# Single-token attention mixed with an MLP: one row of wo moves from SP's queue to GpSimd's, and the GpSimd transfers become eleven

## The chip, the core and the metric

The kernel runs on one core of a Trainium2 chip. The core has a matrix engine (PE, with a separate loader of weights, PEld), a vector engine (DVE), a scalar engine (ACT), a general engine (POOL, or GpSimd) and SP, which only issues transfers. Sixteen DMA engines move data between the chip's memory and the core's SBUF of 128 partitions. The metric is the device time of one execution in microseconds, the median of several.

## The reference: what is computed

One token `x` of 512 values goes through two branches, and a gate mixes them.

```python
g = sigmoid((x * gate_w).sum(-1))
# branch a: 32 heads of 128, a cache of 4096 keys and values for each head
q = (x @ wq).reshape(1, 1, 32, 128)
p = softmax(q . k_cache * 128 ** -0.5)
a = (p . v_cache).reshape(1, 1, 4096) @ wo
# branch b
b = relu(x @ w1 + b1) ** 2 @ w2 + b2
out = g * a + (1 - g) * b
```

All inputs are bf16. The caches of keys and values have 32 MB each, `wq` and `wo` 4 MB each, `w1` and `w2` 1.4 MB each. Every byte is read once and used for one token, and the profile counts 78.35 MB read.

## The kernel before

**Tiles and stages.** The heads are taken in `NT` = 8 groups of four. A group's keys or values are one tile of 128 partitions by 16384 elements (4 MB), one of five slots of `ring`. Each partition holds 32 KB of one head. For a group, DVE multiplies one part of the key blocks with the query and sums (`ttr`, L711), and PE transposes the other part (L509), which ACT copies (L415) and PE multiplies with the query (L522). Then come the maximum, the exponentials on ACT (L434) and the products with V on PE (`pv`, L553).

**The order of the loads.** SP's queue first brings `wq` into `W` (L294). Then it goes through `LOADS`: K0, K1, K2, V0, then K3, V1 and so on. Ahead of each load `free` waits until the slot's former tile has been used. Ahead of the fifth entry, K3, SP waits in `started` until the queries are done, since then `W`, which held `wq`, is free for `wo`. The values of the last three groups come in parts (`PARTS`, L331), with a semaphore each. `w1` and `w2` (L336, L337) come before the last values. The last things on SP's queue are the wo rows of the last four heads (`wob`, L339), the last 128 rows of `w2` (L341) and, at the end, the store of the output (L343).

**Where wo lies.** The first 28 heads' part of `wo` is 3584 rows of 512. It is held as 112 rows of 16384 elements, 32 KB each, on 112 of the 128 partitions of `W`; which row lies on which partition is free, because a matrix of ones and zeros, `selA`, spreads the heads' outputs to match. GpSimd builds `selA` with one `affine_select` for each strip of rows.

A strip is a transfer of `k` rows to `k` partitions at a step. The code counts the sixteen DMA engines as `e` = 0 to 15. Its function `place` turns a kind, an engine, a number of engines, an offset `r` and a multiple `m` into the first partition, the step and the number of rows: `INNER` is 32 + 4e + r, `OUTER` is 4e + r for e below 8 and 64 + 4e + r from 8 on. So the code counts eight partitions as an engine's own: four `INNER` and four `OUTER`. `SEAM` joins partition 28 + r with 96 + r (engines 7 and 8), and `WRAP` joins r with 124 + r (engines 0 and 15).

There are two lists. `FIRST` is issued by SP, ahead of K3, on the semaphore `s_wr` (L327): seven strips of three rows, on engines 0 to 2, and one strip of a single row, `(OUTER, 4, 1, 3, 1)`, which is partition 19. `RUNS` is issued by GpSimd (L378): fourteen strips, each with a semaphore of its own from `s_wp`. A GpSimd transfer of `k` rows takes the next `k` engines from a cursor. To bring the cursor to `e`, `turns` counts how far it has to move, and GpSimd issues a small transfer into `dm` of as many rows (L375); seven of them are issued. A row in a GpSimd strip goes as two pieces of 16 KB (`max_dma_last_dim=16384`).

By these lists, rows for each engine before: engines 0, 1 and 2 have eight each on their own partitions (seven from `FIRST`, one from `RUNS`), engine 3 has none, 4 to 6 and 9 to 14 have seven, and 7, 8 and 15 have eight. The single row of partition 19 is counted for none of these; partition 19 is one of those that the code counts as engine 4's.

**Who waits for wo.** After its last issue GpSimd waits for all `dm` and `wo` transfers and then writes `tick` (L386). PE (`spread_a`) and DVE (`rows_v`) wait for that. PE multiplies 22 of the 32 row columns of `W` (L580) and DVE takes the other ten (L773, L777). PE adds DVE's sum (L586), the last group's `pv` follows, then `norm` (L741), the last four heads' wo (`out_b`, L614) and the last part of w2 (`mlp_out`, L605). DVE adds the bias (L814), PE turns the result (L667), DVE copies it (L816) and SP stores it.

Of the kernel before, what the change touches and what calls it, by code (L numbers as in the profile page):

```python
# [5 lines left out]
def bass_gated_mix__gqa_block_cached__dense_activation_squared_relu__decode_kernel(  # L6
# [50 lines left out]
    for i in (28, 29, 30):  # L57
# [19 lines left out]
    TV = 10  # L77
    TP = 32 - TV
    TM = 6
    INNER, OUTER, SEAM, WRAP = range(4)  # L80
    RUNS = [(INNER, 4, 12, 0, 2), (INNER, 4, 12, 1, 2),
            (OUTER, 4, 3, 0, 1), (SEAM, 7, 2, 0, 1), (OUTER, 9, 7, 0, 1), (OUTER, 4, 3, 1, 1),
            (SEAM, 7, 2, 1, 1), (OUTER, 9, 7, 1, 1), (OUTER, 4, 3, 2, 1),
            (SEAM, 7, 2, 2, 1), (OUTER, 9, 7, 2, 1),
            (SEAM, 7, 2, 3, 1), (WRAP, 15, 2, 3, 1), (OUTER, 1, 2, 3, 1)]
    FIRST = [(INNER, 0, 3, 0, 1), (INNER, 0, 3, 1, 1), (INNER, 0, 3, 2, 1), (INNER, 0, 3, 3, 1),
             (OUTER, 0, 3, 0, 1), (OUTER, 0, 3, 1, 1), (OUTER, 0, 3, 2, 1),
             (OUTER, 4, 1, 3, 1)]

    def place(kind, e, k, r, m):  # L90
        if kind == INNER:
            return 32 + 4 * e + r, 4 // m, k * m
        if kind == OUTER:
            return (4 * e if e < 8 else 64 + 4 * e) + r, 4, k
        if kind == SEAM:
            return 28 + r, 68, k
        return r, 124, k

    def turns():
        at, out = 0, []  # L100
        for _, e, k, _, _ in RUNS:
            d = (e - at) % 16
            out.append((False, d) if d != 1 else (True, e))
            at = (e + k) % 16
        return out

    def strips():
        q = 0
        for run in RUNS + FIRST:
            yield (*place(*run), q)  # L110
            q += place(*run)[2]
        assert q == 4 * NA

    STRIPS = list(strips())
# [4 lines left out]
    woa_v = A_wo.rearrange("(p t) n -> p (t n)", t=32)  # L119
# [15 lines left out]
    with ctx:  # L135
        def sb(name, shape, dt):
            return ctx.enter_context(nc.sbuf_tensor(name, shape, dt))
# [4 lines left out]
        def sem(name):  # L142
            return ctx.enter_context(nc.semaphore(name))
# [3 lines left out]
        def held(kind, j=0):  # L147
            return ring[:, AT[kind, j] % SLOTS, :]

        W = sb("W", [128, 32 * DM], bf16)  # L150
# [90 lines left out]
        s_wp = [sem(f"s_wp{n}") for n in range(len(RUNS))]  # L241
        s_dm = [sem(f"s_dm{n}") for n in range(len(RUNS))]
        s_wr = sem("s_wr")
# [56 lines left out]
        def free(eng, n):  # L300
            if n < SLOTS:
                return
            kind, j = LOADS[n - SLOTS]
            if kind == "k":
                eng.wait_ge(s_sd, U * (j + 1))
                eng.wait_ge(s_t, 2 * U * (j + 1))
            elif kind == "v":
                eng.wait_ge(s_pv, U * (j + 1))

        def started(eng):
            eng.wait_ge(s_qps, NT)
            eng.wait_ge(s_g, 4)
            eng.wait_ge(s_b1c, 1)

        @block.sync
        def _(eng):
            for n, (kind, j) in enumerate(LOADS):
                free(eng, n)  # L320
                if n == SLOTS - 1:
                    started(eng)
                    for p, st, k, q in STRIPS[len(RUNS):]:
                        a, b = W[p:p + st * (k - 1) + 1:st, :], woa_v[q:q + k, :]
                        if k == 1:
                            a, b = [v.rearrange("p (a n) -> p a n", a=2) for v in (a, b)]
                        eng.dma_start(a, b).then_inc(s_wr, 16)  # L327
                if kind == "v" and j in PARTS:
                    for w in range(len(PARTS[j]) - 1):
                        part = slice(PARTS[j][w] * 128, PARTS[j][w + 1] * 128)  # L330
                        eng.dma_start(held("v", j)[:, part], v_v[j][:, part]).then_inc(s_vl[j, w], 16)  # L331
                elif kind in "kv":
                    eng.dma_start(held(kind, j), (k_v if kind == "k" else v_v)[j])\
                       .then_inc(s_l[n % SLOTS], 16)
                elif kind == "m":
                    eng.dma_start(held("m")[:, 0:W2], w1_v).then_inc(s_w[0], 16)  # L336
                    eng.dma_start(held("m")[:, W2:W3], w2_v).then_inc(s_w[1], 16)  # L337
            for c in range(len(TS) - 1):
                eng.dma_start(wob_sb[:, TS[c]:TS[c + 1], :], wob_v[:, TS[c]:TS[c + 1], :])\  # L339
                   .then_inc(s_wo[c], 16)  # L340
            eng.dma_start(w2b, B_w2[F - 128:F, :]).then_inc(s_w[2], 16)  # L341
            eng.wait_ge(s_f4, 1)
            eng.dma_start(out[0, 0, :].rearrange("(j p) -> j p", p=128), fin4).then_inc(s_out, 16)  # L343

        @block.gpsimd
        def _(eng):
            eng.memset(ident[:, :], 0.0).then_inc(s_id, 1)
            eng.memset(identf[:, :], 0.0).then_inc(s_id, 1)
            eng.memset(onesf[:, :], 1.0).then_inc(s_cst, 1)  # L350
            eng.wait_ge(s_id, 2)
            for m in (ident, identf):
                eng.affine_select(out=m[:, :], in_=m[:, :], compare_op=ALU.not_equal, fill=1.0,
                                  base=0, pattern=[[-1, 128]], channel_multiplier=1)\
                   .then_inc(s_id, 1)
            eng.memset(RS[:, :], 0.0).then_inc(s_cst, 1)
            eng.memset(E[:, :, :, :], 0.0).then_inc(s_cst, 1)
            eng.memset(selA[:, :, :], 0.0).then_inc(s_sel, 1)
            eng.wait_ge(s_sel, 1)
            for n, (p, st, k, q) in enumerate(STRIPS):  # L360
                eng.wait_ge(s_sel, n + 1)
                part = selA[:, :, p:p + st * (k - 1) + 1]
                eng.affine_select(out=part, in_=part, compare_op=ALU.not_equal, fill=1.0, base=-st * q,
                                  pattern=[[st, 4], [-1, st * (k - 1) + 1]], channel_multiplier=4 * st)\
                   .then_inc(s_sel, 1)

            started(eng)
            sent = 0
            for n, ((back, d), run) in enumerate(zip(turns(), RUNS)):  # L370
                if back:
                    eng.inc_swdge_sem([], [], mode="reset_dge_cursor")
                if d:
                    src = B_w1[0:d, 0:32].rearrange("p (a c) -> p a c", a=2)
                    eng.dma_start(dm[0:d, sent, :, 0:4], src[:, :, 0:4]).then_inc(s_dm[sent], 16)  # L375
                    sent += 1
                p, st, k, q = STRIPS[n]
                eng.dma_start(W[p:p + st * (k - 1) + 1:st, :], woa_v[q:q + k, :],  # L378
                              max_dma_last_dim=16384).then_inc(s_wp[n], 16)
            for n in range(sent):  # L380
                eng.wait_ge(s_dm[n], 16)
            eng.wait_ge(s_wr, 16 * len(FIRST))
            for q in s_wp[:-1]:
                eng.wait_ge(q, 16)
            eng.wait_ge(s_wp[-1], 16)
            eng.memset(tick[:, :], 0.0).then_inc(s_wk, 1)  # L386
# [461 lines left out]
```

## Time and profile before

| | |
|---|---|
| runs | 193.02, 193.01, 193.13 us; median 193.02 |
| profiled execution | 192.9 us, of it a span of 191.5 us from the first to the last instruction |
| busy, share of the span | DVE 83%, PE 58%, PEld 51%, ACT 43%, POOL 12% |
| DMA | 78.74 MB in 5488 packets, mean 411 GB/s |
| granted PE clock | 0.581 in the mean |
| SP's wo transfers (L327) | 8, issued from 33.5 us on, 411 to 806 ns each |
| GpSimd's wo transfers (L378) | 14, issued from 34.5 to 45.5 us, 556 to 615 ns each |

The page gives busy times of the engines, then the span in 40 slices with one digit each (9 is 90% or more busy), then the DMA queues: q1 has what SP issues, q0 what GpSimd issues, q10 what ACT issues, and q8 and q14 fetch instructions. The chain of waits follows the work that ended last back in time. A row of the timeline has its start, its length, engine, line, operation, tiles, shapes, and in brackets how long the engine was idle before it and what ended that.

### The profile page before, as it was taken

The page shows a single profiled execution, that of the slowest core. Times are in us where ns is not written, and L with a number is a line of the kernel's source. Part 1 is how long each engine was busy: PE and PEld are TensorE (multiplying, and loading weights), DVE is VectorE, ACT ScalarE, POOL GpSimd, SP SyncE. Part 2 cuts the span into 40 slices and gives each one's busy share as a digit, 9 for nine tenths or more (in the row PEclk, how much of TensorE's full clock was granted, in tenths as well). Part 3 has the DMA queues.
Part 4 walks back from the last instruction along what each step waited for, and adds up shares of the span by engine and source line. Part 5 has one row for each costly group of instructions (what it writes and reads, how often), then busy time and mean ns, then how long its engine had stood idle before and what let it go on. Part 6 is the DMA issues. An engine that isn't in the chain of part 4 may idle for free.

```text
span 191.5 us, 6005 instructions
## 1 busy us (share of the span) xinstructions
PE 111.0 (58%) x2058; PEld 97.6 (51%) x2058; DVE 159.0 (83%) x1387; ACT 82.7 (43%) x204; POOL 22.7 (12%) x56
## 2 busy tenths in 40 slices
PE   0129667545614653397569145933887478648975
PEld 0123335535503542297459145933877268537964
DVE  0320399999999999899999998998999799998821
ACT  2105765843833663087349222941663393000400
POOL 7760000996000000000000000000000000000000
PEclk9999985855555555555555555555555555555555
DMA  6999999999999999999999999999999999999992
GB/s 226 432 438 438 438 440 428 438 411 450 411 443 411 421 412 421 438 429 431 414 447 421 428 426 428 431 417 424 428 419 424 411 428 409 421 415 428 417 382 70
DMA packets 5488, 78.74 MB, mean 411 GB/s; under 512 B 1285, under 2 KB 1927, under 8 KB 2056
## 3 DMA queue, kind: packets, MB, share of 16 engines
q1 hardware_dynamic: 4484, 75.40, 92.9%
q0 software_dynamic: 960, 2.95, 3.9%
q8 instruction: 16, 0.26, 0.6%
q14 instruction: 14, 0.11, 0.1%
q10 hardware_dynamic: 14, 0.01, 0.0%
HBM read 78.35 MB, written 0.00 MB: 409 GB/s over the span
## 4 chain that ended last, share of the span: by engine, by line
DVE 48%; DMA 40%; SPq 7%; PE 3%; issue 1%; DVEq 0%
DVE ring L711 45%; DMA ring<-in_A_k_cache_dram 26%; DMA ring<-in_A_wo_dram 14%; SPq L331 6%; DVE S L711 2%; PE pO L553 1%; PE KP L509 1%; DVE gm L725 1%; DVE gx L728 0%; PE pM L562 0%; PE pM L534 0%; PE pQ L614 0%; SPq L337 0%; SPq L294 0%; DVE mp L718 0%
## 5 line engine op out<-in xcount | busy, mean ns | idle before, releaser
L711 DVE CUSTOM_DVE_ANT_0 ring<-ring,qb 128x128 bf16<-128x128 bf16 x656 | 140.6, 280 | 2.9 <-DMA ring<-in_A_k_cache_dram 2.9
L415 ACT ACTIVATE kT<-KP 128x768 bf16<-128x768 bf16 (+1 forms) x64 | 46.4, 783 | 48.1 <-PE KP L509 47.8
L509 PE MATMUL KP<-ident,ring 128*128 128x128 bf16 x368 | 43.4, 302 | 23.2 <-DMA ring<-in_A_k_cache_dram 19.9
L711 DVE DVE_READ_ACCUMULATOR2_ANT S<- 128x1 f32 x656 | 49.7, 76 | 0.1
L509 PEld LDWEIGHTS KP<-ident,ring 128*128 128x128 bf16 x368 | 36.0, 140 | 25.9 <-DMA ring<-in_A_k_cache_dram 20.4
L553 PE MATMUL pO<-E,ring 128*128 128x4 bf16 x640 | 19.5, 167 | 2.9 <-DMA ring<-in_A_v_cache_dram 1.9
L553 PEld LDWEIGHTS pO<-E,ring 128*128 128x128 bf16 x640 | 18.7, 105 | 3.4 <-DMA ring<-in_A_v_cache_dram 2.1
L434 ACT ACTIVATE E<-S,nM 32x128 bf16<-32x128 f32 x32 | 18.5, 580 | 0.9
L553 PE MATMUL pX<-E,ring 128*128 128x4 bf16 x384 | 12.0, 167 | 4.6 <-DMA ring<-in_A_v_cache_dram 4.6
L553 PEld LDWEIGHTS pX<-E,ring 128*128 128x128 bf16 x384 | 11.4, 105 | 5.1 <-DMA ring<-in_A_v_cache_dram 4.9
L426 ACT ACTIVATE nM<-pM 128x1 f32<-128x1 f32 x8 | 1.4, 172 | 23.0 <-PE pM L534 23.0
L529 PE MATMUL pM<-identf,mp 128*1 128x128 f32 x8 | 3.1, 384 | 13.0 <-DVE mp L718 13.0
L534 PE MATMUL pM<-onesf,gx 1*128 1x1 f32 x16 | 4.6, 357 | 8.9 <-DVE gx L728 8.9
L534 PEld LDWEIGHTS pM<-onesf,gx 1*128 1x128 f32 x16 | 4.0, 306 | 9.6 <-DVE gx L728 9.6
L522 PE MATMUL pQ<-qcol,kT 128*128 128x4 bf16 x176 | 7.8, 170 | 1.0 <-ACT kT L415 0.9
L522 PEld LDWEIGHTS pQ<-qcol,kT 128*128 128x128 bf16 x176 | 7.6, 111 | 1.4 <-ACT kT L415 1.4
L434 ACT ACTIVATION_READ_ACCUMULATOR E<-S,nM 32x1 f32 x32 | 8.1, 253 | 0.0
L522 PE MATMUL pS<-qcol,kT 128*128 128x4 bf16 x192 | 8.1, 169 | 0.0
L386 POOL MEMSET tick<- 1x1 f32 x1 | 0.1, 88 | 66.8 <-DMA W<-in_A_wo_dram 66.8
L378 POOL DMA_DIRECT2D W<-in_A_wo_dram x14 | 8.0, 572 | 0.0
L529 PEld LDWEIGHTS pM<-identf,mp 128*1 128x1 f32 x8 | 0.7, 92 | 14.2 <-DVE mp L718 14.0
L522 PEld LDWEIGHTS pS<-qcol,kT 128*128 128x128 bf16 x192 | 7.8, 108 | 0.2
(83 smaller groups left out, 97.3 us busy)
## 6 DMA issues: line engine op xcount, KB each, us to landing
ring<-in_A_k_cache_dram SPq DMA_DIRECT2D x8, 4096.0 KB, 30.4
ring<-in_A_v_cache_dram SPq DMA_DIRECT2D x5, 4096.0 KB, 29.7
W<-in_A_wq_dram SPq DMA_DIRECT2D x1, 4096.0 KB, 12.4
ring<-in_A_v_cache_dram SPq DMA_DIRECT2D x2, 2048.0 KB, 27.7
ring<-in_A_v_cache_dram SPq DMA_DIRECT2D x4, 1024.0 KB, 27.5
ring<-in_A_v_cache_dram SPq DMA_DIRECT2D x2, 1280.0 KB, 31.4
W<-in_A_wo_dram POOLq DMA_DIRECT2D x2, 768.0 KB, 17.8
ring<-in_B_w_dram SPq DMA_DIRECT2D x1, 1376.0 KB, 24.8
```

The costliest lines, as they stand in the source:

```text
L331: eng.dma_start(held("v", j)[:, part], v_v[j][:, part]).then_inc(s_vl[j, w], 16)
L378: eng.dma_start(W[p:p + st * (k - 1) + 1:st, :], woa_v[q:q + k, :], max_dma_last_dim=16384).then_inc(s_wp[n], 16)
L415: eng.activation(kT[:, n % NC, 0:HB[u // U] * 128], KP[n % 3][:, 0:HB[u // U] * 128], ACT.Copy).then_inc(s_ev, 1)
L426: eng.activation(nM[:, j:j + 1], MB[:, j:j + 1], ACT.Copy).then_inc(s_nm, 1)
L434: eng.activation(E[rows, j % NE, :, r], S[rows, j % NS, :], ACT.Exp, bias=nM[rows, j:j + 1], scale=SCALE, accum_out=RS[rows, R * j + r:R * ...
L509: mm = eng.transpose(KP[n % 3][:, y * 128:(y + 1) * 128], held("k", j)[:, b * 128:(b + 1) * 128], ident[:, :])
L522: mm = eng.matmul(S2[j % 2][:, c:c + R], kT[:, n % NC, y * 128:(y + 1) * 128], qcol[:, R * j:R * j + R], start=True, stop=True)
L529: eng.transpose(MT[0:1, :], mp[:, j:j + 1], identf[:, :]).then_inc(s_mt, 1)
L534: eng.matmul(MB[:, j:j + 1], gx[0:1, j % 2, :], onesf[0:1, 0:1], start=True, stop=True).then_inc(s_mb, 1)
L553: mm = eng.matmul(O(R * j, R * j + R), held("v", j)[:, b * 128:(b + 1) * 128], E[:, j % NE, b, :], start=(b == 0), stop=(b == B - 1), skip ...
L711: ins = eng.tensor_tensor_reduce(kb, kb, qb[:, j, :], 1.0, 0.0, ALU.mult, ALU.add, S[:, j % NS, b:b + 1])
L725: eng.tensor_reduce(g, MT[0:1, :].rearrange("a (r p) -> a r p", r=R), AX.X, ALU.max)\
```

## The change

Row strips change place between the lists, and the single rows change their form.

- `FIRST` gets `(OUTER, 0, 3, 3, 1)`, partitions 3, 7 and 11, in place of the single row of partition 19. SP issues eight strips of three rows.
- `RUNS` has eleven strips for fourteen. Offsets 0 to 2 have two `OUTER` strips each, of four and eight rows, for three strips before. Offset 3 has a single row on engine 4 (partition 19), the `SEAM` of 7 and 8, and a single row on engine 15 (partition 127). `WRAP` is gone.
- A single row in `RUNS` goes from GpSimd as one piece of `SOLO` = 16381 elements (a prime number). Its last three elements go from SP, on `s_wr`, so two more transfers of six bytes are issued after the eight strips, and GpSimd waits for `s_wr` to reach 16 x 10.
- There are eight cursor moves through `dm` for seven: six of four rows, one of two, one of six.
- The same 112 partitions are filled, with their rows of wo in another order, and `selA` follows. Rows for each engine on its own partitions after: 0, 1, 2, 4, 7, 8 and 15 have eight, 3 has none, the others seven. The instructions of PE, DVE and ACT are the same, in the same order.

```diff
--- before.py
+++ after.py
@@ -77,24 +77,22 @@
     TV = 10
     TP = 32 - TV
     TM = 6
-    INNER, OUTER, SEAM, WRAP = range(4)
+
+    SOLO = 16381
+    INNER, OUTER, SEAM = range(3)
     RUNS = [(INNER, 4, 12, 0, 2), (INNER, 4, 12, 1, 2),
-            (OUTER, 4, 3, 0, 1), (SEAM, 7, 2, 0, 1), (OUTER, 9, 7, 0, 1), (OUTER, 4, 3, 1, 1),
-            (SEAM, 7, 2, 1, 1), (OUTER, 9, 7, 1, 1), (OUTER, 4, 3, 2, 1),
-            (SEAM, 7, 2, 2, 1), (OUTER, 9, 7, 2, 1),
-            (SEAM, 7, 2, 3, 1), (WRAP, 15, 2, 3, 1), (OUTER, 1, 2, 3, 1)]
+            (OUTER, 4, 4, 0, 1), (OUTER, 8, 8, 0, 1), (OUTER, 4, 4, 1, 1), (OUTER, 8, 8, 1, 1),
+            (OUTER, 4, 4, 2, 1), (OUTER, 8, 8, 2, 1),
+            (OUTER, 4, 1, 3, 1), (SEAM, 7, 2, 3, 1), (OUTER, 15, 1, 3, 1)]
     FIRST = [(INNER, 0, 3, 0, 1), (INNER, 0, 3, 1, 1), (INNER, 0, 3, 2, 1), (INNER, 0, 3, 3, 1),
-             (OUTER, 0, 3, 0, 1), (OUTER, 0, 3, 1, 1), (OUTER, 0, 3, 2, 1),
-             (OUTER, 4, 1, 3, 1)]
+             (OUTER, 0, 3, 0, 1), (OUTER, 0, 3, 1, 1), (OUTER, 0, 3, 2, 1), (OUTER, 0, 3, 3, 1)]
 
     def place(kind, e, k, r, m):
         if kind == INNER:
             return 32 + 4 * e + r, 4 // m, k * m
         if kind == OUTER:
             return (4 * e if e < 8 else 64 + 4 * e) + r, 4, k
-        if kind == SEAM:
-            return 28 + r, 68, k
-        return r, 124, k
+        return 28 + r, 68, k
 
     def turns():
         at, out = 0, []
@@ -321,10 +319,10 @@
                 if n == SLOTS - 1:
                     started(eng)
                     for p, st, k, q in STRIPS[len(RUNS):]:
-                        a, b = W[p:p + st * (k - 1) + 1:st, :], woa_v[q:q + k, :]
+                        eng.dma_start(W[p:p + st * (k - 1) + 1:st, :], woa_v[q:q + k, :]).then_inc(s_wr, 16)
+                    for p, st, k, q in STRIPS[:len(RUNS)]:
                         if k == 1:
-                            a, b = [v.rearrange("p (a n) -> p a n", a=2) for v in (a, b)]
-                        eng.dma_start(a, b).then_inc(s_wr, 16)
+                            eng.dma_start(W[p:p + 1, SOLO:], woa_v[q:q + 1, SOLO:]).then_inc(s_wr, 16)
                 if kind == "v" and j in PARTS:
                     for w in range(len(PARTS[j]) - 1):
                         part = slice(PARTS[j][w] * 128, PARTS[j][w + 1] * 128)
@@ -375,11 +373,13 @@
                     eng.dma_start(dm[0:d, sent, :, 0:4], src[:, :, 0:4]).then_inc(s_dm[sent], 16)
                     sent += 1
                 p, st, k, q = STRIPS[n]
-                eng.dma_start(W[p:p + st * (k - 1) + 1:st, :], woa_v[q:q + k, :],
-                              max_dma_last_dim=16384).then_inc(s_wp[n], 16)
+                a, b = W[p:p + st * (k - 1) + 1:st, :], woa_v[q:q + k, :]
+                if k == 1:
+                    a, b = a[:, 0:SOLO], b[:, 0:SOLO]
+                eng.dma_start(a, b, max_dma_last_dim=16384 * (1 + (k == 1))).then_inc(s_wp[n], 16)
             for n in range(sent):
                 eng.wait_ge(s_dm[n], 16)
-            eng.wait_ge(s_wr, 16 * len(FIRST))
+            eng.wait_ge(s_wr, 16 * (len(FIRST) + sum(run[2] == 1 for run in RUNS)))
             for q in s_wp[:-1]:
                 eng.wait_ge(q, 16)
             eng.wait_ge(s_wp[-1], 16)
```

## The prediction

> **What bounds the kernel now.** I read first the slices of the page, then its queues, then the chain of waits, then the timeline of the end, and last the single transfers.
>
> ```profile
> span 191.5 us, 6005 instructions
> DVE  0320399999999999899999998998999799998821
> DMA  6999999999999999999999999999999999999992
> q1 hardware_dynamic: 4484, 75.40, 92.9%
> q0 software_dynamic: 960, 2.95, 3.9%
> q8 instruction: 16, 0.26, 0.6%
> q14 instruction: 14, 0.11, 0.1%
> ```
>
> The DMA row stands at 9 from the second slice to the last but one: the sixteen engines that move data never rest, while DVE, the busiest compute engine, falls to 2 and 1 at the end. q1 is what SP issues, q0 what GpSimd issues, q8 and q14 fetch instructions.
>
> The end of the chain of waits (window from 185 us), the waits of the last PE groups, and the timeline rows of those groups:
>
> ```profile
> 162.59 25.97 DMA ring<-in_A_wo_dram
> 188.56 0.14 issue
> 188.70 0.57 PE pQ L614 x16
> 189.26 0.28 PE pQ L605 x4
> ...
> 186.71 1.44 PE L553 MATMUL pO<-E,ring 128*128 128x4 bf16 x48 [0.66 <-DMA ring<-in_A_v_cache_dram]
> 188.26 0.22 DVE L741 SCALAR_TENSOR_TENSOR onorm<-pO,gcol,rden 128x4 bf16<-128x4 f32 x1 [5.10 <-PE pO L553]
> 188.67 0.51 PEld L614 LDWEIGHTS pQ<-onorm,ring 128*128 128x128 bf16 x16 [0.60 <-DVE onorm L741]
> ```
>
> Every late step waits for data: the last values of V before 186.71, then wo for the last heads, then the last rows of w2. These three come down one queue in this order. So the question is which DMA engine is last, and why.
>
> The views name no engine, but the trace keeps the sixteen arrivals of each completion semaphore, and each packet with start, length, size and queue. The w2 rows' semaphore arrives at 189.22 from the last engine, 188.79, 188.77, 188.75, 188.70, 188.54, 188.45 and 188.38 from the next seven, 188.0 and earlier from eight. Packets can be strung into sixteen engines, since one starts 3 to 4 ns before the former's end, and since the order of sizes on each engine follows from the code (the counts agree: 960 on q0). Strung so, no engine is idle between 2 us and its own last packet. What an engine carries is its finish. Last packets end:
> - engine 0: 188.80. It carries nine rows of wo (32 KB each), eight on its own partitions and the lone row of partition 19.
> - engines 5, 6 and 9 to 14: seven rows each and the fetches of q8, two each before their data end for seven of them (187.94, 188.02, 188.06, 188.23, 188.35, 188.35, 188.36), one for the eighth (186.8).
> - engines 1, 2, 7, 8, 15 (eight rows): 186.2 to 187.56. Engine 3 (no row, eleven fetches of q14): 187.27. Engine 4 (seven rows): 185.93.
>
> The tail shows in the windows table (columns: stretch, length, busy PE, PEld, DVE, ACT, POOL, clock, DMA share, GB/s):
>
> ```profile
> 187.80:188.20 0.40, 0.35 (x14) 0.27 (x10) 0.00 (x0) 0.00 (x0) 0.00 (x0) 0.50 0.44 151
> 188.20:188.36 0.16, 0.00 (x0) 0.00 (x0) 0.10 (x1) 0.00 (x0) 0.00 (x0) 0.50 0.25 83
> 188.36:188.80 0.44, 0.10 (x4) 0.13 (x5) 0.12 (x1) 0.00 (x0) 0.00 (x0) 0.50 0.20 58
> ```
>
> A share of 0.25 is four engines. In the last row 0.946 us of the 0.20 x 16 x 0.44 = 1.41 us is the sixteenth q8 fetch, which starts at 188.36; the 0.46 left is one engine. For the last 0.44 us only engine 0 still brings data.
>
> **The lone row's price.** A 32 KB packet on q1 takes 1.213 us (median of 1814). The lone row starts at 60.02 and takes 1.919; the packet behind it takes 1.521, 0.308 too long. Together 2.23 us of engine 0. In the same microseconds engine 4 has a 16 KB packet of 1.260 (median 0.611) and a 32 KB packet of 1.726: 0.65 + 0.51 = 1.16 us lost, one row's time, though it carried none. Two engines writing one group of partitions took turns. [...]
>
> **The change part by part.**
> - Engine 0 loses the lone row (-2.23) and its GpSimd row of partition 3 (two packets of 0.611, -1.22), and gets an eighth row from SP (+1.21). It also gets the two three-element remainders: the nearest rows are the 4-byte packets (0.009) and the 2.75 KB one (0.109), with a semaphore packet each, so 0.04 to 0.24 us for two; I take 0.05, as they are nearest to 4 bytes. New end: 188.80 - 2.23 - 1.22 + 1.21 + 0.05 = 186.6. Even at ten times the upper price it would be the last engine only just.
> - Engine 4 gets the row (+1.21) and loses the quarrel (-1.16): 186.0; if the quarrel isn't given back, 187.1. Hidden by the fetch engines' 188.3 either way. Engine 15 trades two packets of 0.611 for one of 1.213, engines 1 and 2 likewise the other way: nothing.
> - The fetch engines keep rows and fetches. GpSimd's queue holds, on each engine, 51 packets for 60 (8 cursor moves of 2, two runs of 5, six of 3, one of 3, two lone rows of 2; before 7 of 2, two of 5, twelve of 3). Nine small ones fewer, 5.5 ns net each, up to 12 with the 1.220 us that the packet behind one may take: -0.05 to -0.11, I take -0.08. New end 188.36 - 0.08 = 188.28.
> - SP issues eight transfers of 0.65 us and two of 0.41 (the lone row's own issue) for seven and one: +1.06 us before the next K load, which starts at 38.98. At that time each engine still has all of the third K and first V loads ahead (landing 45.4 and 58.3), so nothing runs dry. GpSimd issues 19 DMAs for 21 at some 0.57 to 0.61: 1.2 us sooner, and its selector fills are eleven plus eight for fourteen plus eight; all end before the 46 us at which it only waits:
>
> ```profile
> POOL tick L386 <- DMA W<-in_A_wo_dram: 66.8, 1, 66.8
> ```
>
> That wait ends at 112.9 and W is first needed at 173.9, so a wait for two more SP transfers, long landed, costs nothing, and no other instruction is queued behind it.
>
> **The sum.** The last engine's end goes from 188.80 to 188.28 (0.52). The compute chain needs the same: V's third last part lands at 186.67 from engine 0 and 186.28 from the next, so PE starts 0.39 to 0.47 sooner (it has been idle 0.66), and its 1.44, the norm and 0.57 follow; then the w2 group starts at about 188.80 for 189.26. Upstream the same shift: the last K load ends DVE's wait at 151.63 and lands 0.58 sooner without engine 0 (arrivals 151.61 and 151.03), and DVE has slack there:
>
> ```profile
> 132.22 0.29 DVE L711 CUSTOM_DVE_ANT_0 ring<-ring,qb 128x128 bf16<-128x128 bf16 x1 [0.80 <-DMA ring<-in_A_k_cache_dram]
> 151.63 0.29 DVE L711 CUSTOM_DVE_ANT_0 ring<-ring,qb 128x128 bf16<-128x128 bf16 x1 [0.51 <-DMA ring<-in_A_k_cache_dram]
> ```
>
> So -0.46 us. This is against the profiled execution (192.9, span 191.5), which lies 0.12 under the median; taken off the median 193.02 it gives 192.56. Its bounds: -0.30 when two q8 fetches of the worst engine fall at the longest seen (1.142 for a median of 1.069, 0.15 in all), -0.60 when they fall short. What is late next is the instruction fetch group, not data of wo: of the 2.2 us taken from engine 0 only 0.46 can be seen.
>
> **The rivals.**
> - Same: the gain is there on engine 0, but the fetch group or the PE chain ends later than in this execution. For it: seven engines lie within 0.42 us, and the end is their largest. Against it: their two fetches each are PE's own program, which doesn't change. Gain 0.1 to 0.35, about 192.8.
> [...]
> - Slower: the lone rows of 1 x 16381 don't stay on one engine but are spread over sixteen. Then all sixteen write one group of partitions and take turns, so each loses about one row's 1.21 us, twice: fetch group 188.28 + 2.4 = 190.7, 1.9 over 188.80, time 194.9. It decides as soon as each row costs the fetch engines over 0.26 us. For it: no GpSimd transfer of one row is in the trace. Against it: SP's lone row, of the same form, raised its semaphore from one engine and is one 32 KB packet. [...]
> - The change doesn't do what it says: the row goes to another engine than 4, say 5, which writes across again: 188.28 + 2.23 = 190.5, time 194.7. Against it: the fourteen runs before fit the cursor's order packet for packet.
>
> **How the numbers follow.** About 0.2% (0.39 us, so 192.63) is what a measurement of this kernel can tell from no change. The forecast has 0.73; by its bounds (-0.30 to -0.60, most near -0.46) 0.62 of it is faster by more, 0.11 within. The same rivals have 0.14, of it 0.02 the rule's; spread rows 0.09, wrong engine 0.04. So faster 0.62, same 0.25, slower 0.13. The forecast's own range is 192.42 to 192.72; to hold 8 in 10 it reaches up into the same rivals, 192.35 to 192.88, and leaves out the slower ones.
>
> **What would show it.** Packets: q0 51 x 16 = 816, 2.88 MB; q1 some 4492. No 32 KB packet of 1.9 us near 60 us. Arrivals of the w2 rows: no lone last engine; the last group near 188.7, all fetch engines. In the windows of the end the last stretch holds two or more engines. GpSimd's wait ends near 102, nine packets of some 1.2 us sooner. The last K load releases DVE near 151.0. The forecast is wrong if one lone row shows as sixteen arrivals' delay (every engine 1 us late near 100 us), or if the tail is as long with another engine last.

## The result and the profile after

The changed kernel takes 195.36 us (median of 4) for 193.01 of the kernel before: a ratio of 1.012, interval 1.0109 to 1.0132. It is slower by 2.35 us, where 0.46 less was forecast. The profiled execution took 195.38 us, its span grew from 191.5 to 194.0.

The page of the changed kernel, span and DMA queues:

```profile
span 194.0 us, 5998 instructions
DMA  6999999999999999999999999999999999999970
q1 hardware_dynamic: 4492, 75.47, 92.0%
q0 software_dynamic: 816, 2.89, 3.8%
```

The packets are those forecast (816 and 4492), and the DMA row still stands at 9 from the second slice on. But the last two slices read 7 and 0 for 9 and 2: the end has become a long tail in which few engines work. The end of the chain of waits, and the waits of GpSimd and DVE:

```profile
163.84 27.20 DMA ring<-in_A_wo_dram
191.04 0.14 issue
191.17 0.56 PE pQ L614 x16
...
191.74 0.28 PE pQ L605 x4
...
POOL tick L386 <- DMA W<-in_A_wo_dram: 58.5, 1, 58.5
DVE ring L711 <- DMA ring<-in_A_k_cache_dram: 5.6, 5, 1.7
```

The two last PE groups are as long as before and begin 2.5 us later, behind the same transfers. GpSimd's wait ends at 102.7, as forecast, so its side is not late. DVE waits 5.6 us for K where it waited 2.9 (`DVE ring L711 <- DMA ring<-in_A_k_cache_dram: 2.9, 4, 1.4` before), and these two rows of its timeline answer to 132.22 and 151.63 of before:

```profile
134.63 0.29 DVE L711 CUSTOM_DVE_ANT_0 ring<-ring,qb 128x128 bf16<-128x128 bf16 x1 [0.82 <-DMA ring<-in_A_k_cache_dram]
154.06 0.29 DVE L711 CUSTOM_DVE_ANT_0 ring<-ring,qb 128x128 bf16<-128x128 bf16 x1 [0.53 <-DMA ring<-in_A_k_cache_dram]
```

Already at 134 us the last engine's share of K is 2.4 us later than before. So the loss lies ahead of that, and is carried to the end by one engine. The windows table of the tail (stretch, length, busy PE, PEld, DVE, ACT, POOL, clock, DMA share, GB/s) says how many:

```profile
189.60:190.10 0.50, 0.50 (x25) 0.50 (x22) 0.00 (x0) 0.00 (x0) 0.00 (x0) 0.50 0.06 23
190.90:191.30 0.40, 0.13 (x5) 0.16 (x6) 0.05 (x1) 0.00 (x0) 0.00 (x0) 0.50 0.06 20
```

0.06 of sixteen is one engine. The arrivals of the last w2 rows agree: 191.70, then 190.12, then 189.05 and thirteen earlier ones. Before they were 189.22, 188.79, 188.77.

Which engine? The two single rows can be found on q0 by their size of 32762 bytes: they start at 69.90 and 81.95. At 69.9 us an engine that has GpSimd rows to carry stands at the 25th of its 51 q0 packets, and the first single row is the 41st. Only engines 0, 1 and 2, whose q0 packets are nearly all of four bytes, are so far ahead. Strung together as in the prediction, all packets of this trace fit only if **both single rows run on engine 0, and the first of them doesn't move the cursor**; with the first single row on engine 4, 1 or 2, with the second on engine 15, or with a cursor that the first one moves, the strings break off. (The second is GpSimd's last strip, so nothing behind it could show whether it moves the cursor.) The packets of engines 0, 1 and 2 are alike in this kernel but for single rows; that the string is engine 0's agrees with SP's two six-byte pieces, also for one partition each, which stand on it at 61.28 and 61.31. Engine 0 then ends at 191.27, 2.47 later than before. The next arrival of the w2 rows is 1.6 us ahead of its own.

So engine 0, which had one row of another engine's partitions, now has two: partition 19 and partition 127. It carries ten rows, and engines 4 and 15, for which the lists count eight, carry seven. And the strip behind the first of them, partitions 31 and 99, runs on engines 6 and 7 where the code counts 7 and 8.

### The profile page after: what moved, and what is told of

It is laid out like the page before. It is cut to its first block, busy times and chain, and to the rows that moved or that the text cites. A ratio compares the mean times of both kernels' runs of the same rounds, so it can differ in the third digit from the quotient of the medians.

```text
span 194.0 us, 5998 instructions
## 1 busy us (share of the span) xinstructions
PE 109.2 (56%) x2058; PEld 96.8 (50%) x2058; DVE 159.0 (82%) x1387; ACT 82.9 (43%) x204; POOL 19.8 (10%) x51
## 3 DMA queue, kind: packets, MB, share of 16 engines
q1 hardware_dynamic: 4492, 75.47, 92.0%
## 4 chain that ended last, share of the span: by engine, by line
DMA 60%; DVE 30%; SPq 6%; PE 3%; issue 1%
DMA ring<-in_A_k_cache_dram 46%; DVE ring L711 27%; DMA ring<-in_A_wo_dram 14%; SPq L329 5%; DVE S L711 1%; PE pO L553 1%; PE KP L509 1%; DVE gx L728 0%; DVE gm L725 0%; PE pM L534 0%; PE pQ L614 0%; SPq L335 0%; SPq L292 0%; SPq L334 0%; PE pS L522 0%
## 5 line engine op out<-in xcount | busy, mean ns | idle before, releaser
L711 DVE CUSTOM_DVE_ANT_0 ring<-ring,qb 128x128 bf16<-128x128 bf16 x656 | 140.6, 281 | 5.6 <-DMA ring<-in_A_k_cache_dram 5.6
L509 PE MATMUL KP<-ident,ring 128*128 128x128 bf16 x368 | 42.8, 299 | 29.3 <-DMA ring<-in_A_k_cache_dram 26.1
L509 PEld LDWEIGHTS KP<-ident,ring 128*128 128x128 bf16 x368 | 35.4, 138 | 31.7 <-DMA ring<-in_A_k_cache_dram 26.5
L711 DVE DVE_READ_ACCUMULATOR2_ANT S<- 128x1 f32 x656 | 50.8, 77 | 0.1
L406 ACT ACTIVATE qb<-pQ 32x128 bf16<-32x128 f32 x16 | 4.3, 268 | 6.7 <-PE pQ L487 6.4
L373 POOL DMA_DIRECT2D dm<-in_B_w_dram x8 | 5.0, 620 | 21.0 <-PE pX L487 21.0
L777 DVE SCALAR_TENSOR_TENSOR ring<-W,o2f,ring 128x512 f32<-128x512 bf16 x9 | 6.8, 751 | 0.3
```

Source lines behind the costliest of these rows:

```text
L406: eng.activation(qb[rows, c, :], QR[c % 2][rows, r * 128:r * 128 + 128], ACT.Copy)\
L509: mm = eng.transpose(KP[n % 3][:, y * 128:(y + 1) * 128], held("k", j)[:, b * 128:(b + 1) * 128], ident[:, :])
L711: ins = eng.tensor_tensor_reduce(kb, kb, qb[:, j, :], 1.0, 0.0, ALU.mult, ALU.add, S[:, j % NS, b:b + 1])
L777: eng.scalar_tensor_tensor(out=vsum[:, :], in0=wo_sb[:, TP + t, :], scalar=o2f[:, t:t + 1], in1=vsum[:, :], op0=ALU.mult, op1=ALU.add).the ...
```

## The experiments

Theory L: a GpSimd transfer to one partition runs on the lowest engines, whatever the cursor says, and leaves the cursor. With it, Q: such a row is dear since it is written beside the partitions' owner, which is the engine that the code counts them for and that writes there at the same time. The rivals were the regrouping of the strips (R) and the odd size of 16381 elements (S). The diffs are cut to the lines that carry the point, and said to be against the kernel before, the regrouped one or the changed one. Each ratio is to the kernel before, run on the same chip.

**The regrouping alone.** Against the kernel before:

```diff
-            (OUTER, 4, 3, 0, 1), (SEAM, 7, 2, 0, 1), (OUTER, 9, 7, 0, 1), ...
+            (OUTER, 4, 4, 0, 1), (OUTER, 8, 8, 0, 1), ...
             (SEAM, 7, 2, 3, 1), (WRAP, 15, 2, 3, 1), (OUTER, 1, 2, 3, 1)]
```

> The kernel before with the strips of offsets 0 to 2 regrouped into fours and eights alone (eleven runs; partition 19 stays with SP). Theory L (in the changed kernel both single GpSimd rows run on engine 0 and leave the cursor where it was): rows per engine as before, so engine 0 stays last with SP's lone row, 192.9 to 193.0 us. Rival R (the regrouping costs the time): 195.3.

Measured: 192.81 us, against 192.92 for the kernel before on the same chip, ratio 0.9997 (0.9989 to 1.0006). R falls; eleven strips for fourteen cost nothing and save nothing that can be measured.

**One single row from GpSimd.** This is the move of partition 19 by itself, against the regrouped kernel. The row's last three elements go from SP, as in the changed kernel.

```diff
+            (WRAP, 15, 2, 3, 1), (OUTER, 1, 2, 3, 1), (SEAM, 7, 2, 3, 1), (OUTER, 4, 1, 3, 1)]
-             (OUTER, 4, 1, 3, 1)]      # of FIRST, SP's list
```

> The regrouped kernel, and of the single rows only partition 19 goes from GpSimd as 16381 elements, as its last run; partition 127 stays in the strip with partition 3. Theory L: engine 0 carries eight own rows and one lone row of 1.9 us and what follows it, as before: 193.0, within 0.15. Rival S (the row runs on engine 4, and only the odd size is slow, 1.93 for 1.21): engine 0 ends at 186.6 and engine 4 at 187, the fetch engines bound: 192.55.

Measured: 192.87 us, ratio 1.0003 (0.9994 to 1.0011). It is L's number, and S's 192.55 lies outside. Moving the row from SP to GpSimd changed who issues it and not which engine carries it: engine 0's last packet ends at 188.76, before at 188.80. From this kernel to the changed one engine 0 ends 2.51 us later, and the second single row is what it gets.

**A single row on engine 0's own partition.** Against the changed kernel; its two single rows are gone from GpSimd's list:

```diff
+            (SEAM, 7, 2, 3, 1), (OUTER, 1, 4, 3, 1), (OUTER, 0, 1, 3, 1)]
-             (OUTER, 0, 3, 3, 1)]      # of FIRST
```

> One single GpSimd row of 16381 elements, as its last run, on partition 3, which the code counts as engine 0's own; SP has seven strips, GpSimd's strip of four takes partitions 7, 11, 15 and 19 on engines 1 to 4, engine 15 keeps seven rows. Theory L (a GpSimd transfer to one partition runs on the lowest engines, here engine 0) with Q (what is slow is writing beside the owner): the row's packet takes 1.21 to 1.22 us, engine 0 ends near 186.5, engine 3 bounds at 188.5: 192.72, within 0.15, as without any single row. Rival S (the odd size is slow): the packet takes 1.93 us, engine 0 ends near 187.3, same time.

Measured: 192.76 us, ratio 0.9990 (0.9979 to 1.0001). The packet decides between Q and S. The DMA view of a window of 0.02 us in which the row starts has its length as a share of sixteen engines, so length = share x 16 x 0.02 us. First the changed kernel at 69.90 us, then this one at 83.30:

```profile
q0 software_dynamic: 1, 0.03, 603.4%
```

```profile
q0 software_dynamic: 1, 0.03, 379.1%
```

1.931 us across, 1.213 on the own partition, with the same 16381 elements. S falls: the size cost nothing. In this kernel the only slow packet within 3 us of it stands behind an instruction fetch (1.859 us at 84.74), while in the changed one engine 4 has one of 2.03 us at 70.0 and engine 15 one of 1.81 at 81.8 (median 1.21). So what was slow was the writing beside the partitions' owner: both times the engine that the code counts as the owner had a slow packet in the same microseconds.

**The cursor.** The changed kernel, with a count that leaves single rows out; the diff is against the changed kernel.

```diff
-            at = (e + k) % 16
+            at = (e + (k if k > 1 else 0)) % 16
```

> The changed kernel, but its count of the cursor leaves a single row out (a move of three rows for two). Theory L: the cursor was one behind, so now the strip of partitions 31 and 99 runs on engines 7 and 8; the slow packets near 94 to 97 us go; the last but one arrival of the w2 rows falls from 190.1 to about 189.0; engine 0 still carries both single rows and is last: 195.3, within 0.15. If a single row does move the cursor: the strip runs on 8 and 9 and writes across, the last but one arrival stays near 190.

Measured: 195.17 us, ratio 1.0107 (1.0091 to 1.0123). The last arrivals are 191.40, 188.88, 188.84: the second last fell from 190.12 to 188.88 as L says, the slow packets near 94 to 97 us are gone (one of 1.70 at 94.96 is left, behind a fetch of q8), and engine 0 is still last. So the cursor did stay behind the first single row, and the strip on the wrong engines was a second loss, hidden under the first.

**The single rows whole.** Here a row of 16384 elements from GpSimd went as sixteen pieces of 1024: the page of this kernel has 161 packets from 2 to 8 KB, that of the changed one 129. Against the changed kernel; SP's two remainders and the wait for them are gone too.

```diff
-    SOLO = 16381
+    SOLO = 16384
```

> The changed kernel with the two single rows whole, which then go as sixteen pieces of 1024 elements each. Theory L with Q: sixteen engines take a piece each; engines 0 to 2 come to it near 70 us, the others near 95 us nearly at once and take turns on one group of partitions, so each loses 0.1 to 1.2 us a row: engine 0 is not last, the fetch engines bound at 188.3 + 0.2 to 2.4: 192.8 to 195.0, I take 193.3. If all pieces run on engine 0: 195.3 or later.

Measured: 194.43 us, ratio 1.0065 (1.0046 to 1.0083), inside the wide range, but not at 193.3 and not for the reason given. All sixteen engines carry pieces, of 0.084 us mostly and 0.235 at most, so sharing a row over all engines was cheap here. Engine 0's end is one of three, at 187.2, 187.5 and 188.4, for engines 0 to 2. What bounds is engine 6 or 7 at 190.25. It carries fetches, and by the wrong cursor one of the rows of partitions 31 and 99 too. In the changed kernel the next to last arrival, 190.12, was this loss, hidden under engine 0. How much of the 190.25 it makes no run shows, since none has whole rows and a right cursor.

**The row in two pieces.** 16382 elements as two pieces of 8191, the cursor set to engine 3. Against the regrouped kernel:

```diff
+            (SEAM, 7, 2, 3, 1), (WRAP, 15, 2, 3, 1), (OUTER, 1, 2, 3, 1), (HALF, 3, 2, 3, 1)]
```

> The regrouped kernel, with partition 19's row from GpSimd in two pieces of 8191 elements as a transfer of two, cursor at engine 3 (so engines 3 and 4), two elements left to SP. Theory L: a transfer of two follows the cursor, engine 0 has eight rows and ends near 186.6, engine 3 ends at 187.3 + 0.61 + at most 0.5 for the quarrel with engine 4: the fetch engines bound at 188.3, time 192.55, range 192.45 to 192.75. If every transfer to one partition runs on engine 0 whatever its pieces: 193.0. Rival S: 192.55 as well, with pieces of 0.95 us for 0.61.

Measured: 192.88 us, ratio 0.9999 (0.9990 to 1.0008): a miss. The pieces start at 85.52 and 88.38, 0.676 and 0.766 us long. The strings fit with the pieces on engines 0 and 1, and break with 3 and 4. So two pieces didn't save it: here too the transfer to one partition ran on the lowest engines. Engine 0 ended at 187.4 and engine 1 at 188.54. But in this execution one fetch engine ended at 188.65, so engine 1 alone doesn't explain why nothing was gained; that stays open.

**No single row at all.** Against the kernel before. The strips are regrouped as in the first experiment, GpSimd's strips of partitions 3 and 127 and of 7 and 11 are gone, and partition 15 is filled in place of 127.

```diff
             (OUTER, 0, 3, 0, 1), (OUTER, 0, 3, 1, 1), (OUTER, 0, 3, 2, 1),
-             (OUTER, 4, 1, 3, 1)]
+             (OUTER, 0, 5, 3, 1)]
```

> No single row at all: SP's offset-3 strip has five rows on engines 0 to 4 (partitions 3, 7, 11, 15, 19), GpSimd has nine runs, engine 15 keeps seven rows. Both theories: engine 0 has eight rows and ends near 186.6, engine 3 gets one row, 187.3 + 1.2 = 188.5, the fetch engines end at 188.3: 192.7, range 192.55 to 192.8. It shows what the lone row costs when nobody writes across.

Measured: 192.72 us against 192.92, ratio 0.9991 (0.9982 to 1.0000). The packets fit with one row of SP's strip on each of engines 0 to 4, so partition 19 is written by engine 4, and from 4 us on no row's packet is slow but those behind instruction fetches. Engine 0's share, so far the latest, is among those that end by 186.9; engine 3 ends at 188.46 and the fetch engines at 188.26 at most. The chain's end:

```profile
188.38 0.57 PE pQ L613 x16
188.94 0.28 PE pQ L604 x4
```

For 188.70 and 189.26 before. This is the change's aim, partition 19 written by its owner, without a single row. It is worth some 0.1%, at the edge of what can be measured. Against the changed kernel it is some 2.5 us, each taken against its own runs of the kernel before.

## Why the prediction was wrong

- **What bounds** held: sixteen saturated engines, the last of them sets the end. So did the identity of engine 0, its 188.80, and the price of a row written across: 2.23 us before, and 1.931 + 0.361 and 1.929 + 0.336 for the two after (the second term is what the packet behind takes over 1.213).
- **"Engine 4 gets the row" and "Engine 15 trades two packets of 0.611 for one of 1.213"** are the steps that failed. Neither engine got its row; engine 0 got both. With the right engine the prediction's own terms give the result: 186.6 for engine 0 without single rows, plus twice its 2.23, is 191.1, and with the measured 2.29 and 2.27 it is 191.2; measured 191.27. The strip that ran one engine too low is a second loss that the prediction has no term for; it ended 1.6 us ahead of engine 0 and set nothing.
- **The rival that names this** ("the row goes to another engine than 4") was there, with a chance of 0.04. The evidence set against it was bad: the fourteen GpSimd strips fit the cursor, but each had two rows or more, and none was a transfer to one partition. The one such transfer in the trace, SP's, ran on engine 0. The nearest row spoke for the rival. Its 194.7 was short of 195.36, since only one of the two rows was moved in it.
- **The spread of the rows over sixteen engines**, the rival given the larger chance, did not happen at 16381 elements. With the rows whole it did happen, and cost far less than its 2.4 us: at most 0.235 us a piece.
- **The chance of 0.02 called "the rule's"** stands on a rule that no run shows. What the runs showed is one case in which the issuer did not matter: the move of partition 19's row from SP to GpSimd by itself changed nothing (192.87 us, ratio 1.0003), because engine 0 carried it both times.
- **The size of the gain** of 0.46 was not put to the test, as no run has the change's rows on the engines it names. The nearest, five rows on SP, gained 0.20 us in the medians, interval 0 to 0.35. The bound on the fetch engines was too tight: their last end lay between 188.26 and 188.66 in the executions where it could be read and no strip ran on wrong engines, where 0.15 either way was allowed for.

## What to carry to other kernels

When all DMA engines are saturated, count the bytes for each engine, and add what it writes beside another engine's partitions: here each such row cost its engine 2.23 to 2.29 us, and the slowest engine set the time. That a queue places transfers in a known way is shown only for the shapes that were seen; a new shape, here one partition for several, needs its own look at where it lands. The two fastest forms tried, 192.72 and 192.76 us and the same within their intervals, have no row written beside its owner; one of them gets there by a strip wide enough to reach the owner.

## What was not expected of the hardware

- A GpSimd transfer to one partition ran on engine 0 (one piece, at 69.90 and 81.95 us in the changed kernel), on 0 and 1 (two pieces, at 85.52 and 88.38), or on all sixteen (sixteen pieces, of 0.235 us at most). Where a strip of two partitions came behind it, it had not moved the cursor that the strips of two and more partitions followed: with single rows left out of the count, the second last arrival fell from 190.12 to 188.88.
- Two engines writing into what the code counts as one engine's eight partitions slowed each other: 32 KB took 1.919 us in the kernel before, 1.931 and 1.929 in the changed one, for 1.213, and the owner lost about as much as a row takes (1.16 us in the kernel before; the slow packets of engines 4 and 15 in the changed one, with the 16 KB packets behind them, give 1.23 and 1.19).
- The sixteen instruction fetches of q8, 16 KB each, took 0.946 to 1.142 us in the kernel before (median 1.069) and 1.018 to 1.276 in the changed one (median 1.072). In the kernel before they fell on eight of the engines, two for seven of them and one for the eighth before their data ended, and of the fourteen of q14 eleven fell on engine 3. With two q8 fetches before its data end, an engine of the eight ended some 3 us later than its seven rows alone would make it. This is an estimate from the kernel before: engines 7, 8 and 15, without a fetch, end near 186.2 with eight rows, so near 185.0 with seven, and those with two fetches at 187.9 to 188.4. In the kernel without single rows, where engine 0 is relieved, they ended at 188.26 at most, next to engine 3 with its one row (188.46).
